# One core, eight batches of attention and experts: the first batch's loads and sums in another order

## The chip, the core and the metric

The kernel runs on one core of a Trainium2 chip. A core has TensorE (PE, matmuls; its weight loads are shown apart as PEld), VectorE (DVE), ScalarE (ACT), GpSimd (POOL) and SyncE (SP). SyncE here only issues DMA transfers; ScalarE issues a few at the start. Each queue works in its own order, and waits at an instruction until all that it needs is there. The metric is the device time of one execution in microseconds (us), as a median of several runs.

## What is computed

For each of 8 batches and 8 heads, 576 positions are mapped onto 32 memory slots by a softmax of `phi`; keys and values of the slots are weighted sums over the positions; each query attends to the 32 slots. The heads side by side make a token of 512 numbers. A router picks one of 8 experts for each token, and the expert is two matrices with a ReLU between, scaled by the router's probability.

```python
a = softmax(phi, axis=2)                       # [8, 8, 576, 32]
k_m = einsum('bhsm,bhsd->bhmd', a, k)          # 32 slots of 64 for each head
v_m = einsum('bhsm,bhsd->bhmd', a, v)
x = softmax(q @ k_m.T / 8) @ v_m               # then [4608, 512]
logits = unit(x) @ unit(expert_emb).T / tau
e, gate = argmax(logits), max(softmax(logits))
out = gate * (relu(x @ w1[e]) @ w2[e])         # all in float32
```

## The kernel before

The host lays the inputs out: `phiT` has 4 heads times 32 slots on 128 partitions (two groups `g` of four heads), `kv` holds keys and values of 512 positions side by side, and `kvt` those of the last 64.

The program is written out by hand; every engine gets its instructions in the order of the code, and nothing reorders them. For each batch b:

- `load_phi` brings the two maps (288 KB each) to `ex`. `largest` takes the negated maximum of a row on VectorE (L393), `softmax` the exponential on ScalarE with its sum (L407), `shares` the reciprocal of the sums on VectorE (L418, L422).
- `turn` transposes the exponentials on TensorE in blocks of 128 positions (L428), and ScalarE copies them to `eT` (L429).
- `load_kv` brings keys and values: four pieces of 128 positions, `kx0` to `kx3`, 512 KB each, and the last 64 positions, `kl`, 256 KB on 64 partitions.
- `slots(b, g)` sums them on TensorE: for one group of heads, five pieces k = 0 to 4 of four products each into one accumulator (L440). Group 0 of the first batch has the accumulator `acc`, group 1 another, `acc1`.
- `block` scales the sums with the shares, keys to `kb` (VectorE, L459), values to `vb` (ScalarE, L461). `flip` transposes them (L469) and copies them to `kT` and `vT` (L472). `score` then multiplies keys and queries (L485); `load_q` has brought the queries in two halves of 576 KB, the first for group 0 and the second for group 1.
- `Tokens` turns scores into attention, tokens and the choice of an expert: `fill`, `weigh`, `divide`, `turn`, `attend`, `choose`. The chosen expert's `w1` and `w2` are loaded only then (L378, L384).
- `project`, `first` and `second` are the expert's matmuls, and most of TensorE's work. The next batch's steps are threaded between them by `steps`.

For the first batch there is nothing to thread into. The entry function writes its steps one after the other: `warm` keeps TensorE busy with matmuls of a constant, then loads, constants, softmax and the router (a generator in three parts: the square of the embedding on ScalarE, a square root by iteration on VectorE, the transposes on TensorE). The DMA issues of the start stand on two queues: SyncE has the maps, `kx0` to `kx3`, then the queries; ScalarE has `kl`, the embedding `emb` and `tau`. The program gives its DMA transfers eight semaphores in turn, so that the ninth waits for the first to land: here `kx3` waits for `kl` (L359).

## Time and profile before

| what | us |
|---|---|
| three runs | 423.91, 424.69, 425.17 |
| median | 424.69 |
| the profiled execution | 424.73 |
| its span, first to last instruction | 422.9 |
| TensorE busy in it | 406.7 |

Times in the rows below are microseconds from the start of the span, of the one profiled execution. A row of the timeline has start, duration, engine, line, operation, what it writes and reads with shapes, how many instructions were merged (x4), and in brackets the idle time of the engine before it and what ended that. A letter q behind an engine (SPq, ACTq) marks its queue issuing a DMA; the landing comes later. Matmuls in float32 take several passes and are recorded more than once each.

### The profile page before, as it was taken

The page shows a single profiled execution, that of the slowest core. Times are in us where ns is not written, and L with a number is a line of the kernel's source. Part 1 is how long each engine was busy: PE and PEld are TensorE (multiplying, and loading weights), DVE is VectorE, ACT ScalarE, POOL GpSimd, SP SyncE. Part 2 cuts the span into 40 slices and gives each one's busy share as a digit, 9 for nine tenths or more (in the row PEclk, how much of TensorE's full clock was granted, in tenths as well). Part 3 has the DMA queues.
Part 4 walks back from the last instruction along what each step waited for, and adds up shares of the span by engine and source line. Part 5 has one row for each costly group of instructions (what it writes and reads, how often), then busy time and mean ns, then how long its engine had stood idle before and what let it go on. Part 6 is the DMA issues. An engine that isn't in the chain of part 4 may idle for free. (4 is left out here: it accounts for less than half of the span.)

```text
span 422.9 us, 9359 instructions
## 1 busy us (share of the span) xinstructions
PE 406.7 (96%) x3485; PEld 329.1 (78%) x3485; DVE 258.7 (61%) x830; ACT 169.2 (40%) x462; POOL 167.5 (40%) x195
## 2 busy tenths in 40 slices
PE   7779899999999999999999999999999999999994
PEld 2448778688887978879786888879788797869784
DVE  5698796569673695547772696736955476645000
ACT  4465732365223632257313652236322571045110
POOL 1021471295133921268131951339212681339100
PEclk9999999999999999999999999999999999999998
DMA  8989925996769924995469926699349504592011
GB/s 264 354 320 338 359 60 134 315 348 246 154 202 405 330 48 112 352 359 222 69 195 379 340 109 146 209 404 331 50 112 345 193 2 87 163 380 69 15 50 55
DMA packets 67570, 91.19 MB, mean 216 GB/s; under 512 B 40792, under 2 KB 45656, under 8 KB 67520
## 3 DMA queue, kind: packets, MB, share of 16 engines
q1 hardware_dynamic: 64720, 82.00, 58.8%
q0 software_dynamic: 2688, 8.26, 5.5%
q8 instruction: 29, 0.48, 0.4%
q10 hardware_dynamic: 112, 0.28, 0.2%
q14 instruction: 21, 0.17, 0.1%
HBM read 71.19 MB, written 19.33 MB: 214 GB/s over the span
## 5 line engine op out<-in xcount | busy, mean ns | idle before, releaser
L579 PE MATMUL ph<-aT,gh 128*128 128x288 f32 x512 | 105.7, 300 | 1.7 <-DVE hl L585 1.1
L632 PE MATMUL py<-wh,hh 128*128 128x512 f32 x248 | 102.0, 411 | 0.0
L632 PE MATMUL py<-wh,hl 128*128 128x512 f32 x248 | 97.1, 391 | 0.0
L632 PE MATMUL py<-wl,hh 128*128 128x512 f32 x248 | 96.8, 390 | 0.0
L550 POOL TENSOR_TENSOR wl<-w2s,wh 128x512 fp32r<-128x512 f32 x64 | 83.4, 1306 | 19.1 <-DMA kx<-kv 12.7
L579 PEld LDWEIGHTS ph<-aT,gh 128*128 128x128 f32 x512 | 81.3, 188 | 5.6 <-DVE gl L563 2.6
L579 PE MATMUL ph<-aT,gl 128*128 128x288 f32 x256 | 75.3, 294 | 0.0
L585 DVE SCALAR_TENSOR_TENSOR hl<-ph,hh 128x288 fp32r<-128x288 f32 x128 | 55.7, 449 | 28.0 <-ACT hh L582 21.2
L637 ACT ACTIVATE ys<-py,gate 128x512 f32<-128x512 f32 (+1 forms) x39 | 25.0, 640 | 107.9 <-PE py L632 50.9
L582 ACT ACTIVATE hh<-ph 128x288 fp32r<-128x288 f32 x128 | 51.7, 416 | 30.0 <-PE ph L579 28.3
L736 POOL DMA_DIRECT2D out_dram<-ys x28 | 15.5, 553 | 109.2 <-ACT ys L637 101.6
L632 PEld LDWEIGHTS py<-wh,hh 128*128 128x128 f32 x248 | 46.6, 188 | 12.1 <-issue 4.3
L632 PEld LDWEIGHTS py<-wh,hl 128*128 128x128 f32 x248 | 46.5, 188 | 10.2
L632 PEld LDWEIGHTS py<-wl,hh 128*128 128x128 f32 x248 | 46.7, 188 | 8.1
L579 PEld LDWEIGHTS ph<-aT,gl 128*128 128x128 f32 x256 | 48.0, 188 | 0.0
L540 POOL TENSOR_TENSOR aT<-aw,aT 128x576 fp32r<-128x576 f32 (+3 forms) x20 | 23.8, 1205 | 48.8 <-PE py L632 35.8
L563 DVE TENSOR_TENSOR gl<-pg,gh 128x512 fp32r<-128x512 f32 x32 | 20.0, 684 | 36.3 <-ACT gh L562 36.2
L549 POOL CAST wh<-w2s 128x512 fp32r<-128x512 f32 x56 | 37.5, 670 | 0.0
L621 PE MATMUL py<-w2s,h 128*64 128x256 f32 x256 | 29.4, 382 | 0.0
L119 DVE TENSOR_REDUCE lg<-po 128x8 f32<-128x16 f32 x40 | 6.8, 174 | 30.4 <-PE po L114 30.4
L621 PEld LDWEIGHTS py<-w2s,h 128*64 128x64 f32 x256 | 17.7, 137 | 9.3 <-issue 1.3
L114 PEld LDWEIGHTS po<-vv,aw 128*128 128x128 f32 x160 | 21.8, 189 | 3.5 <-ACT vv L526 1.0
(154 smaller groups left out, 506.2 us busy)
## 6 DMA issues: line engine op xcount, KB each, us to landing
kx<-kv SPq DMA_DIRECT2D x32, 512.0 KB, 7.3
w2s<-w SPq DMA_DIRECT2D x32, 512.0 KB, 9.8
w1s<-w SPq DMA_DIRECT2D x28, 512.0 KB, 5.2
qt<-qT SPq DMA_DIRECT2D x14, 576.0 KB, 7.7
out_dram<-ys POOLq DMA_DIRECT2D x28, 256.0 KB, 6.0
ex<-phiT SPq DMA_DIRECT2D x16, 288.0 KB, 10.1
ad<-aw SPq DMA_DIRECT2D x8, 576.0 KB, 12.6
td<-x SPq DMA_DIRECT2D x56, 72.0 KB, 2.2
```

The source lines that it names most:

```text
L114: nc.tensor.matmul(po[:, 144 * g : 144 * g + P + E], lhsT=k.aw[:, g, to], rhs=k.vv[:, g], start=True, stop=True)
L540: self.nc.gpsimd.tensor_tensor(out=al, in0=a, in1=ah.bitcast(F32), op=ALU.subtract)
L549: (copy or self.nc.scalar.copy)(h, x)
L550: self.nc.gpsimd.tensor_tensor(out=l, in0=x, in1=h.bitcast(F32), op=ALU.subtract)
L563: nc.vector.tensor_tensor(out=self.gl[:, g, f], in0=ps[g], in1=self.gh[:, g, f].bitcast(F32), op=ALU.subtract)
L579: nc.tensor.matmul(p, lhsT=w[:, g, fs], rhs=x[:, g, to], start=g == 0 and k == 0, stop=g == 1 and k == 2)
L582: nc.scalar.activation(self.hh[:, f, to], p, AF.Relu)
L585: nc.vector.scalar_tensor_tensor(out=self.hl[:, f, to], in0=p, scalar=0.0, in1=self.hh[:, f, to].bitcast(F32), op0=ALU.max, op1=ALU.subtract)
L621: nc.tensor.matmul(p[64 * j : 64 * j + 64], lhsT=self.h4[:, f], rhs=self.w2s[:, f, d * j : d * j + d], start=f == 0, stop=f == 7,)
L632: nc.tensor.matmul(p, lhsT=h[:, f, to], rhs=w[:, f], start=f == 0 and k == 0, stop=f == 7 and k == 2)
L637: nc.scalar.activation(y[:, :d], p, AF.Copy, scale=gate[:, i : i + 1])
L736: eng.dma_start(self.out[r : r + P], y)
```

## The change

It touches the first batch alone.

- The loads: `load_router` (emb, tau) is issued ahead of keys, values and queries. The keys and values follow in it: `kx1` on ScalarE's queue, `kx0`, `kx2`, `kx3` and then `kl` on SyncE's. Queries come after that.
- An exponential of one constant per partition is put on ScalarE behind its loads, so that the table of exponentials is loaded there.
- The router's square comes ahead of the exponentials, its square root ahead of the shares. Both maxima are taken before either share, and the shares of both groups after the transposes, with one reciprocal.
- The sums of both groups are interleaved by piece: pieces 0 and 1 of group 0, then of group 1, then piece 2 of both, piece 3 of both, piece 4 (`kl`) of both. Both `block` steps come behind that.

```diff
@@ load_router
         nc.scalar.dma_start(self.tv, self.tau.broadcast_to((E, 1)))
+        self.load_kv(0)
+        nc.scalar.activation(st([P, 1], F32, name="e8"), self.ones[:, :1], AF.Exp)
@@ load_kv
-        if b < B:
-            (self.nc.sync if b else self.nc.scalar).dma_start(self.kl[:64], self.kvt[b])
+        if not b:
+            for k in range(4):
+                (self.nc.scalar if k == 1 else self.nc.sync).dma_start(self.kx[k], self.kv[b, :, k])
+            self.nc.sync.dma_start(self.kl[:64], self.kvt[b])
+        elif b < B:
+            self.nc.sync.dma_start(self.kl[:64], self.kvt[b])
             for k in range(4):
                 self.nc.sync.dma_start(self.kx[k], self.kv[b, :, k])
@@ slots
-    def slots(self, b, g, acc=None):
+    def slots(self, b, g, acc=None, ks=(0, 1, 2, 3, 4), start=True, stop=True):
...
-        for k in range(5):
+        for k in ks:
...
-                    start=k == 0,
-                    stop=k == 4,
+                    start=start and k == ks[0],
+                    stop=stop and k == ks[-1],
@@ moe_linformer
     k.load_phi(0)
-    k.load_kv(0)
+    k.load_router()
     k.load_q(0)
-    k.load_router()
     k.consts()
...
     router = k.router()
+    next(router)
     for g in range(NG):
+        k.largest(0, g)
         k.softmax(0, (g,))
-        k.shares(0, (g,))
     next(router)
...
+    k.shares(0)
     k.load_phi(1)
-    next(router)
...
-    k.slots(0, 0)
+    for ks in ((0, 1), (2,), (3,), (4,)):
+        for g in range(NG):
+            k.slots(0, g, acc if g else None, ks, start=0 in ks, stop=4 in ks)
     k.block(0, 0)
-    k.slots(0, 1, acc)
```

In the order of the instructions, two places change. The first is the head of SyncE's queue, here with the semaphores that an issue waits for (`DMAHW0` to `DMAHW7` are the eight of the DMA transfers). Before:

```order
L353 DMA ex<-phiT 128x576 x2
L359 DMA kx_70<-kv 128x1024
L359 DMA kx_71<-kv 128x1024
L359 DMA kx_72<-kv 128x1024
L359 DMA kx_73<-kv 128x1024 [waits DMAHW0_49]
L366 DMA qt<-qT 128x1152 [waits DMAHW1_49]
L366 DMA qt<-qT 128x1152 [waits DMAHW2_49]
```

and in the changed kernel:

```order
L355 DMA ex_69<-phiT 128x576 x2
L360 DMA kx0_70<-kv 128x1024
L360 DMA kx2_72<-kv 128x1024
L360 DMA kx3_73<-kv 128x1024
L361 DMA kl_74<-kvt 64x1024 [waits DMAHW0_49]
L372 DMA qt_75<-qT 128x1152 [waits DMAHW1_49]
L372 DMA qt_75<-qT 128x1152 [waits DMAHW2_49]
```

`kx1` has left this queue and `kl` has come to the end of the keys; `DMAHW0` is `kl`'s own in the kernel before and `emb`'s in the changed one. The queries stand behind both as they did. ScalarE's queue, before, up to the square of the router (L321):

```order
L357 DMA kl<-kvt 64x1024
L311 DMA sT<-emb 8x512
L313 DMA tv<-tau 8x1
L407 ACT_TABLE_LOAD
L407 ACTIVATE ex,sm_149<-ex,nm_148 128x576 x2
L321 ACTIVATE w2s,es<-sT 8x512
```

and in the changed kernel:

```order
L311 DMA sT<-emb 8x512
L313 DMA tv<-tau 8x1
L360 DMA kx_71<-kv 128x1024
L315 ACT_TABLE_LOAD
L315 ACTIVATE e_129<-ones 128x1
L323 ACTIVATE w2s,es<-sT 8x512
L413 ACTIVATE ex,sm_153<-ex,nm_152 128x576 x2
```

The table load has moved from behind the wait for the first map to behind the issues, and the square from behind the exponentials to ahead of them. The second place is on TensorE, the products of the first batch (`acc` is group 0's accumulator, `acc_146` or `acc_148` group 1's; each row is four products). Before:

```order
L440 MATMUL acc<-kx_70,eT 32x128 x4
L440 MATMUL acc<-kx_71,eT 32x128 x4
L440 MATMUL acc<-kx_72,eT 32x128 x4
L440 MATMUL acc<-kx_73,eT 32x128 x4
L440 MATMUL acc<-kl,eT 32x128 x4
L440 MATMUL acc_146<-kx_70,eT 32x128 x4
L440 MATMUL acc_146<-kx_71,eT 32x128 x4
L440 MATMUL acc_146<-kx_72,eT 32x128 x4
L440 MATMUL acc_146<-kx_73,eT 32x128 x4
L440 MATMUL acc_146<-kl,eT 32x128 x4
```

and in the changed kernel:

```order
L446 MATMUL acc<-kx_70,eT 32x128 x4
L446 MATMUL acc<-kx_71,eT 32x128 x4
L446 MATMUL acc_148<-kx_70,eT 32x128 x4
L446 MATMUL acc_148<-kx_71,eT 32x128 x4
L446 MATMUL acc<-kx_72,eT 32x128 x4
L446 MATMUL acc_148<-kx_72,eT 32x128 x4
L446 MATMUL acc<-kx_73,eT 32x128 x4
L446 MATMUL acc_148<-kx_73,eT 32x128 x4
L446 MATMUL acc<-kl,eT 32x128 x4
L446 MATMUL acc_148<-kl,eT 32x128 x4
```

The products are the same forty; those of group 1 have come from behind all of group 0's to right behind its product of the same piece.

## Rows read from the trace of the kernel before

**Rows 1.** The head of the profile's page: the span.

```profile
span 422.9 us, 9359 instructions
```

**Rows 2.** The table by stretch for the first 14 us and for one stretch of the steady part: from and to, its length, then the busy time of each engine (x instructions), the granted clock of TensorE, the busy share of the DMA engines and GB/s.

```profile
0.00:14.00 14.00, 9.89 (x104) 4.83 (x105) 7.30 (x32) 5.31 (x11) 1.73 (x8) 1.00 0.87 302
101.00:152.00 51.00, 51.00 (x445) 41.66 (x446) 33.15 (x105) 20.46 (x57) 21.52 (x24) 1.00 0.70 231
```

**Rows 3.** The waits of TensorE over the whole run, longest in total first: who waited, for whom, us in total, times, the longest.

```profile
PE acc L440 <- DMA kx<-kv: 2.2, 4, 0.9
...
PE ph L579 <- DVE hl L585: 1.1, 1, 1.1
...
PE pg L560 <- DMA w1s<-w: 0.7, 1, 0.7
```

**Rows 4.** The timeline of the first batch, from the first loads to the scores of the second group.

```profile
0.71 0.55 ACTq L357 DMA_DIRECT2D kl<-kvt  x1
...
1.30 0.72 ACTq L311 DMA_DIRECT2D sT<-emb  x1
...
3.86 0.75 DVE L393 TENSOR_REDUCE nm<-ex 128x1 f32<-128x576 f32 x1 [0.85 <-DMA ex<-phiT]
3.91 1.28 ACT L407 ACT_TABLE_LOAD   x1 [3.91 <-DMA ex<-phiT]
...
5.20 0.77 ACT L407 ACTIVATE ex<-ex,nm 128x576 f32<-128x576 f32 x1
...
6.37 0.73 DVE L393 TENSOR_REDUCE nm<-ex 128x1 f32<-128x576 f32 x1
...
7.91 0.62 ACT L321 ACTIVATE w2s<-sT 8x512 f32<-8x512 f32 x1
...
9.13 0.43 PE L440 MATMUL acc<-kx,eT 128*32 128x128 f32 x8 [0.31 <-ACT eT L429]
...
9.75 0.43 PE L440 MATMUL acc<-kx,eT 128*32 128x128 f32 x8 [0.18 <-DMA kx<-kv]
...
11.17 0.47 DVE L328 TENSOR_SCALAR w2s<-sT,en 8x512 f32<-8x512 f32 x1
...
12.27 0.43 PE L440 MATMUL acc<-kx,eT 128*32 128x128 f32 x8 [0.85 <-DMA kx<-kv]
...
12.52 0.40 PE L440 MATMUL acc<-kl,eT 128*32 128x128 f32 x8
...
12.73 1.06 PE L440 MATMUL acc<-kx,eT 128*32 128x128 f32 x32
...
14.08 0.48 DVE L459 TENSOR_SCALAR kb<-acc,rs 128x256 f32<-128x256 f32 x1 [0.61 <-PE acc L440]
...
14.62 0.44 PE L469 MATMUL tf_1True<-ident,kb 128*128 128x128 f32 x2 [0.25 <-DVE kb L459]
...
14.99 0.85 PE L485 MATMUL ts<-qt,kT 64*32 64x128 f32 x16
15.10 0.27 ACT L472 COPY kT<-tf_1True 128x128 f32<-128x128 f32 x1 [0.42 <-PE tf_1True L469]
...
15.42 0.15 PEld L485 LDWEIGHTS ts<-qt,kT 64*32 64x32 f32 x8 [0.27 <-ACT kT L472]
```

**Rows 5.** The table by stretch again (columns as in rows 2), for what the DMA engines moved: before the first maps, up to the landing of `kx3`, right after it, a later stretch with a `kl` in flight, and the stretch behind that.

```profile
0.00:2.00 2.00, 0.97 (x3) 0.42 (x4) 1.11 (x6) 0.00 (x0) 1.36 (x8) 1.00 0.15 26
...
2.00:12.27 10.27, 7.19 (x46) 2.87 (x44) 5.71 (x27) 4.83 (x10) 0.38 (x1) 1.00 0.99 337
...
12.00:14.00 2.00, 1.73 (x57) 1.53 (x58) 0.48 (x1) 0.47 (x1) 0.00 (x0) 1.00 1.02 418
...
40.50:44.00 3.50, 3.50 (x66) 2.88 (x66) 3.19 (x19) 1.84 (x7) 0.00 (x0) 1.00 1.05 244
44.50:48.00 3.50, 2.71 (x21) 2.47 (x19) 2.53 (x8) 3.50 (x15) 1.52 (x2) 1.00 1.02 404
```

**Rows 6.** From issue to landing in us, from the lists of DMA issues and of single tiles: `kl` of the first batch, `kl` of the third; the issue of the two halves of the queries on SyncE's queue; the landing of the first half alone; and shortest, median and longest of the two halves, the longest being the second's.

```profile
kl<-kvt ACTq DMA_DIRECT2D x1, 256.0 KB, 4.7
...
kl<-kvt SPq DMA_DIRECT2D x1, 256.0 KB, 10.9
...
5.75 1.28 SPq L366 DMA_DIRECT2D qt<-qT  x2
...
qt<-qT SPq DMA_DIRECT2D x1, 576.0 KB, 7.9
...
DMA to landing us min/median/max: 7.9/8.3/8.7
```

**Rows 7.** The timeline where the chosen expert's first matrix is issued and where TensorE takes up its second half.

```profile
22.45 1.42 SPq L378 DMA_DIRECT2D w1s<-w  x2
...
31.78 1.09 PE L560 MATMUL pg<-w1s,vT 64*32 64x512 f32 x16 [0.67 <-DMA w1s<-w]
```

**Rows 8.** The timeline of VectorE near 47 us.

```profile
46.47 1.26 DVE L220 TENSOR_SCALAR zz<-zz 128x5 f32<-128x5 f32 x1
```

**Rows 9.** The table by stretch (columns as in rows 2) for a stretch of the start in which TensorE stands idle, and for the end, behind the last matmul.

```profile
24.67:26.00 1.33, 0.00 (x1) 0.00 (x1) 1.06 (x4) 1.33 (x5) 0.00 (x0) 1.00 1.03 363
417.12:419.00 1.88, 0.00 (x1) 0.00 (x0) 0.48 (x1) 0.00 (x0) 0.00 (x0) 1.00 0.22 73
419.00:420.00 1.00, 0.00 (x0) 0.00 (x0) 0.00 (x0) 0.00 (x0) 0.00 (x0) 0.70 0.08 18
```

## The prediction, written before the changed kernel ran

> **What bounds the kernel now.** I first read the span and the table by stage: in the steady part TensorE is busy for 51 us of 51, while the first 14 us leave it 4.1 us idle [rows 1, 2]. So an edit of the first batch can only make the steady part begin earlier or later. The chain that ended last holds one piece, at the very end, and says nothing of the start; the list of waits does. TensorE's longest are those on the keys and values (2.2 us), then one on VectorE's hl (1.1 us) and one on w1 (0.7 us) [rows 3]. In order of time, TensorE has the transposed exponentials at 9.13 and then stands before each piece of keys and values: kx1 at 9.75, kx3 at 12.27. The second group's sums run only after that, its kb is made at 14.08, its keys are turned at 14.62, its copy kT ends at 15.37 (15.10 and 0.27), and the scores of the second group, ts, start at 15.42 [rows 4].
>
> What the keys wait for is bytes, not issue: between 2.00 and 12.27 us the DMA engines are busy for 0.99 of the time at 337 GB/s, and at 418 from 12 to 14 us [rows 5]. Those 10.27 us moved 3.46 MB; maps, keys and values and embedding are 2896 KB, 2.97 MB. So the moved bytes are 0.5 MB, or 1.2 us at 418 GB/s, ahead of what has landed.
>
> One load stands close behind: the second half of q was issued at about 6.4 us (two issues in 1.28 us from 5.75) and took 8.7 us, so it landed at 15.1 us [rows 6]. The scores that need it began at 15.42. That is 0.3 us of slack, and this number decides my forecast.
>
> **The change part by part.** *Exponentials.* The table load of 1.28 us stood at 3.91, behind the wait for the maps, and the first exponential came at 5.20 [rows 4]. In front of it ScalarE now issues three loads, at most 0.72 us each (emb's), and then loads the table: 0.71 + 2.2 + 1.28 = 4.2 us at the latest, before the first maximum can be ready (3.86 + 0.75 = 4.6). An exponential of one element per partition is new, between 0 and the 0.27 us of a 128x128 copy, also before the maximum. The router's square, 0.62 us, now goes ahead of the exponentials instead of behind them, so the first starts at about 5.1, as before or a little earlier. It waits for emb to land, which no row of before shows; even at 7 us both exponentials, 0.77 each, would end before 9.75. The second maximum (6.37) stood behind the first share; it now waits for its map alone, so it is not later. With the square gone from between, the copies of the transposes come about 0.6 us earlier. All of this is covered by kx1, which came at 9.75 [rows 4]: I price it at 0; without that cover it would be 0.3 us, the wait on eT at 9.13, since the next wait is for keys anyway.
>
> *Router and shares.* VectorE's router chain ended at 11.64 (11.17 and 0.47) and now goes ahead of the shares (five small adds and one reciprocal, under 1 us). It could not start before the square's end at 8.5; now it starts once the square and the second maximum are done, by 7.1 (6.37 and its 0.73), 1.4 us earlier, so it ends near 10.2 and the shares are ready near 11.2. Their reader kb cannot run before the last load has landed, at 12.3 (below) [rows 4]. Cover of 1 us, cost 0; at L = 10.3, the low bound below, it would cost 0.9. One reciprocal less on VectorE: 0, off the path.
>
> *Queues.* kx1 moves from SyncE's queue to ScalarE's, kl from the head of ScalarE's to the end of the keys on SyncE's. SyncE's stall at the fourth key load, which waited until kl had landed (0.71 + 4.7 = 5.4), is gone; kl waits for emb instead, and q's first half for the first map, landed at 3.86. With the engines at 0.99 busy, earlier issue moves no byte earlier: 0. The Trainium skill's page "DMA: Bandwidth & Descriptors" (section "Issuing engines are not separate DMA queues") says the same against this edit: loads of several queues run on the same engines, and a second queue saves the issue time alone. The busy share here agrees.
>
> *Order of the sums.* The work of TensorE is the same, but after the last landing L only the kl products of both groups remain. Eight rows took 0.40, and 32 took 1.06, so about 0.27 per group: both done at L + 0.7. Then VectorE makes both kb, 0.48 each, from L + 0.45 to L + 1.45; the turn takes 0.44 and ScalarE's copy 0.27, with waits as before, so ts of the second group may start at L + 2.3. In the old order it started 15.42 - 12.27 = 3.15 after its last landing [rows 4]. That alone is a gain of 0.85 us, if L stays at 12.3.
>
> *L.* The bytes up to kl are those that had landed by 12.27, so I take L = 12.3. Below: all at 418 GB/s gives 2.0 + 7.1 + 1.2 = 10.3. Above: kx3 lands 0.63 earlier (256 KB at 418 GB/s) and kl, which landed 3.4 us after the engines began (0.71 + 4.7 = 5.4; 26 GB/s up to 2 us), takes these 3.4 by itself: 15.0 [rows 4 to 6]. Stretches with a kl in flight are slow, 244 GB/s from 40.5 to 44 against 404 right after, and the kl of a later batch took 10.9 us [rows 5, 6]; this keeps me from the low end, but the same slow stretch is in the 337 GB/s already. The Trainium skill's page "SBUF — State Buffer" (section "Door 1: The DMA port swizzle") says that 64 partitions, which is what kl fills, reach half of the memory's ports and get about 196 GB/s. By that page kl would take, as an estimate, 1.3 us in place of 0.63, L would be near 13.0 and the gain in the sum below 0.1 in place of 0.3; the slow stretches agree in kind.
>
> *q.* It stays behind the same bytes, so it lands at 15.1 again; from 13.0 (4.15 MB at 418 GB/s, 2.0 + 9.9 + 1.1) to 15.7 (0.6 us more, if the slow stretch is longer in its new place) [rows 5, 6].
>
> *Sum.* The second ts starts at the later of L + 2.3 = 14.6 and q = 15.1, so at 15.1 in place of 15.42: a gain of 0.3. With the bounds: 13.0 to 17.3, from 2.4 faster to 1.9 slower.
>
> *To the end.* The scores lead over VectorE's chain to the choice of an expert and so to the issue of w1 (22.45); the second half of w1 lets the projection start at 31.78, where TensorE waited 0.67 us [rows 7]. From there the order fixes the rest. SyncE's later issues (the next batch's keys, released at 14.07 by the last products) come about 1 us earlier; nobody on the path waits for them. So 0.3 us arrives at the end. The profiled execution took 424.73, of which 422.9 is span; 424.73 - 0.3 = 424.4. The median of the three runs, 424.69, is the same within 0.04.
>
> **The rivals.** *A: the DMA gets faster.* If kl at the head of the line is what slowed phi and the keys, everything lands sooner; q at 13.8 and L at 11.5 would give ts at 13.8, a gain of 1.6: 423.1. For it: 337 against 418 GB/s, and the slow stretches go with kl [rows 5]. Against it: kl is still ahead of q, so its slow stretch should only move.
>
> *B: the last load becomes the bound, slower.* kl lands after all keys. From L = 13.1 on, L + 2.3 is later than 15.42 and the change loses. With kl needing its 3.4 us alone, L = 15.0 and the loss is 1.9: 426.6. For it: the 10.9 us of the later kl [rows 6]. Against it: the first kl shared its 3.4 us with both maps, the later one with all that stood ahead in the queue.
>
> *C: the change does nothing.* Its gains are all under the DMA or fall to q, or the keys of the next batch or w1 hold the start in place: 424.7.
>
> *D: the clock.* TensorE would stand idle between the products of kx3 and the landing of kl. The granted clock stayed at 1.00 over an idle stretch of 1.33 us and fell within 419 to 420, some 2 us after the last matmul [rows 9]. If it fell from 2.4 to 1.2 GHz here, the 2.0 us of matmuls from L to the end of ts (0.7, 0.44, 0.85) would take twice as long: +2.0 - 0.3, 426.4. By bytes the idle stretch is about 1 us, so it is unlikely.
>
> *E: the stall at 48 us.* A 128x5 add took 1.26 us on VectorE near 47 us, and TensorE then waited 1.1 us for hl [rows 3, 8]. If a shift of the start breaks up that meeting, 1.1 us come back: 423.3.
>
> **How the numbers follow.** Forecast (gain 0 to 1.0, q bounds) 0.58, A 0.17, B 0.08, C 0.08, D 0.03, E 0.06. About 0.3%, 1.27 us, is what a measurement of this kernel can tell from no change. Faster by that: most of A (0.14), half of E and a small tail of the forecast, 0.20 in all; slower by that: B from L = 14.4 on (0.03), D (0.03) and a tail, 0.08; within it 0.72. For 8 in 10 the range takes the forecast, C, E and the inner part of A and of B: 422.9 to 425.5.
>
> **What would show it.** Right: exponentials end by 7.5; the products of kl are the last for both groups, within 0.8 us; the second ts starts near 15.1 and its wait is on the DMA of q, no longer on ScalarE's copy; w1 is issued near 22.1. A shows itself by q landing before 14.2 and over 380 GB/s from 2 to 12 us; B by kl landing after 13.1 with TensorE waiting for kl longest; D by a granted clock under 1.00 before 20 us; E by no wait on hl near 48. I am wrong if the second ts starts before 14.4 or after 15.6, or if it starts near 15.1 and the span moves by over 1 us all the same.

## The result: 0.75% slower, where a gain of 0.3 us was forecast

| | kernel before | changed kernel |
|---|---|---|
| median, us (18 runs each) | 424.56 | 427.88 |
| lowest to highest | 423.49 to 426.21 | 424.54 to 430.10 |
| the profiled execution | 424.73 | 428.48 |
| its span | 422.9 | 426.7 |

The ratio is 1.0075 with an interval of 1.0054 to 1.0096: slower, outside the range of 422.9 to 425.5.

TensorE's mean granted clock is known for each run (0.988 for the profiled one), and it counts below: a run with 0.994 or more is taken as one in which the clock held through the batches, one with 0.993 or less as one in which it fell for some microseconds. The line is a rough one. The profiles show where the clock was at half: behind the last matmul it takes 0.001 to 0.0065 off the mean of a run, with no cost in the batches, and a fall of 3.4 us within the batches takes only 0.004 (e6's profiled run, counted as held with 0.994, has one). So the counts of falls below are counts by this line. Of the changed kernel's 18 runs 4 held, with a median of 425.43, and 14 fell, with 428.39. The forecast said 424.4. One run of the kernel before, 511.66 us at a clock of 0.75, is left out everywhere.

The head of the changed kernel's page, for [rows 1]:

```profile
span 426.7 us, 9361 instructions
```

Its longest waits of TensorE (who waited, for whom, us in total, times, the longest), for [rows 3]:

```profile
PE acc L446 <- DMA kx<-kv: 2.8, 2, 1.9
PE acc L446 <- ACT vb L467: 1.8, 1, 1.8
PE acc L446 <- DMA kl<-kvt: 1.3, 1, 1.3
PE ph L585 <- DVE hl L591: 1.1, 1, 1.1
...
PE pg L566 <- DMA w1s<-w: 0.9, 1, 0.9
```

A wait on kl, which no row of before has, and a longer one on the keys. Where they lie, the timeline of its first batch tells, for [rows 4]:

```profile
1.63 1.37 SPq L360 DMA_DIRECT2D kx<-kv  x3
...
2.04 1.28 ACT L315 ACT_TABLE_LOAD   x1 [2.04 <-issue]
...
3.04 0.58 SPq L361 DMA_DIRECT2D kl<-kvt  x1
...
4.34 0.77 ACT L413 ACTIVATE ex<-ex,nm 128x576 f32<-128x576 f32 x1 [0.20 <-DVE nm L399]
...
5.52 0.78 ACT L413 ACTIVATE ex<-ex,nm 128x576 f32<-128x576 f32 x1 [0.31 <-DVE eng L38]
...
8.78 1.64 PE L446 MATMUL acc<-kx,eT 128*32 128x128 f32 x48 [0.90 <-DMA kx<-kv]
...
12.32 0.64 PE L446 MATMUL acc<-kx,eT 128*32 128x128 f32 x16 [1.90 <-DMA kx<-kv]
...
14.25 1.08 PE L446 MATMUL acc<-kl,eT 128*32 128x128 f32 x16 [1.29 <-DMA kl<-kvt]
14.97 0.93 DVE L465 TENSOR_SCALAR kb<-acc,rs 128x256 f32<-128x256 f32 x2 [5.79 <-PE acc L446]
...
15.99 0.65 PE L475 MATMUL tf_1True<-ident,kb 128*128 128x128 f32 x2
...
16.67 0.27 ACT L478 COPY kT<-tf_1True 128x128 f32<-128x128 f32 x1 [0.17 <-PE tf_1True L475]
...
16.99 0.20 PEld L491 LDWEIGHTS ts<-qt,kT 64*32 64x32 f32 x8 [0.23 <-ACT kT L478]
```

(acc<-kx and acc<-kl are the products of the sums, kb the scaled keys, tf their transposes, kT the copies of these, ts the scores.) The exponentials are through at 6.3, earlier than before. Then TensorE has the first three pieces from 8.78 on, stands 1.90 us for kx3 and 1.29 us for kl, which comes at 14.25. The second group's scores start at 16.99 in place of 15.42, and wait for the copy kT, not for q. The products of kl took 1.08 us; the same sixteen rows took 0.64 in e2 below, where the clock held. The table by stretch, for [rows 2, 5, 9] (from and to, length, busy time of PE, PEld, DVE, ACT, POOL, granted clock, DMA share, GB/s):

```profile
2.00:12.27 10.27, 7.52 (x70) 4.15 (x68) 5.57 (x26) 5.28 (x11) 0.38 (x1) 1.00 0.99 319
10.00:12.00 2.00, 0.42 (x16) 0.15 (x8) 0.00 (x0) 0.00 (x0) 0.00 (x0) 1.00 1.03 214
12.00:14.00 2.00, 0.64 (x16) 0.38 (x16) 0.00 (x0) 0.00 (x0) 0.00 (x0) 0.88 0.99 297
13.50:20.30 6.80, 5.88 (x60) 3.29 (x68) 3.48 (x8) 2.50 (x9) 0.00 (x0) 0.50 0.95 288
20.30:22.00 1.70, 1.70 (x31) 0.90 (x16) 1.58 (x6) 1.03 (x5) 0.00 (x0) 0.98 1.03 417
```

From 10 to 12 us, with kl in flight behind the keys, the DMA engines are as busy as before and move 214 GB/s, where 12 to 14 us had 418 in the kernel before [rows 5]. TensorE is idle for 2.9 of the 4 us from 10 to 14, and its granted clock goes to 0.50 (1.2 GHz) from 13.5 to 20.3, while kl's products, the transposes and the scores run.

The way on, for [rows 7]: the issue of w1, the projection with its second half (pg), and the first products of the expert's first matrix (ph), which stood at 32.80 in the kernel before:

```profile
24.67 1.40 SPq L384 DMA_DIRECT2D w1s<-w  x2
...
34.38 1.09 PE L566 MATMUL pg<-w1s,vT 64*32 64x512 f32 x16 [0.91 <-DMA w1s<-w]
...
35.40 0.53 PE L585 MATMUL ph<-aT,gh 128*128 128x288 f32 x2
```

So 2.60 of the 3.75 us of the profiled executions are lost before the first ph. The rest: the steady batches take 49.35 us each in place of 49.30, from the start of the same product of the expert's second matrix (py) in the second and the seventh batch, (347.51 - 101.00) / 5 in the kernel before and (350.52 - 103.75) / 5 in the changed one:

```profile
101.00 0.44 PE L621 MATMUL py<-w2s,h 128*64 128x256 f32 x2
...
347.51 0.44 PE L621 MATMUL py<-w2s,h 128*64 128x256 f32 x2
```

```profile
103.75 0.44 PE L627 MATMUL py<-w2s,h 128*64 128x256 f32 x2
...
350.52 0.44 PE L627 MATMUL py<-w2s,h 128*64 128x256 f32 x2
```

With the first and the last batch that makes 0.4; the last matmul starts 3.02 us later (416.84 and 419.86). The remaining 0.7 lies behind it: the span ends 6.1 us after the last matmul's start in the kernel before and 6.8 in the changed one. In the profiles of all the kernels below this end took 6.1 to 8.1 us.

### The profile page after: what moved, and what is told of

It is laid out like the page before. It is cut to its first block, busy times and chain, and to the rows that moved or that the text cites. A ratio compares the mean times of both kernels' runs of the same rounds, so it can differ in the third digit from the quotient of the medians.

```text
span 426.7 us, 9361 instructions
## 1 busy us (share of the span) xinstructions
PE 408.8 (96%) x3485; PEld 331.1 (78%) x3485; DVE 257.9 (60%) x829; ACT 169.5 (40%) x463; POOL 167.5 (39%) x195
## 5 line engine op out<-in xcount | busy, mean ns | idle before, releaser
L638 PEld LDWEIGHTS py<-wh,hh 128*128 128x128 f32 x248 | 46.6, 188 | 12.3 <-issue 4.3
L638 PEld LDWEIGHTS py<-wh,hl 128*128 128x128 f32 x248 | 46.5, 188 | 10.2
## 6 DMA issues: line engine op xcount, KB each, us to landing
ex<-phiT SPq DMA_DIRECT2D x16, 288.0 KB, 10.3
```

The source lines that it names most:

```text
L638: nc.tensor.matmul(p, lhsT=h[:, f, to], rhs=w[:, f], start=f == 0 and k == 0, stop=f == 7 and k == 2)
```

## The experiments

Each was timed beside the kernel before on its own chip. That kernel's median there was 425.1 to 426.5, and by the line above 56 of its 135 runs fell (median 426.4 to 427.1 on the chips) and 79 held (424.8 to 425.0). So the two kinds of run lie some 1.6 to 2.3 us apart, and both happen to the kernel before too. Some expectations put the line at 0.996, which also counts runs as fallen whose only stretch at half clock is the end: e12's profile has a mean of 0.995 and 1.00 all through the start. Ratios are to the kernel before; 95% intervals stand in brackets.

### Where kl stands

**e1_kl_first**: the changed kernel with kl at the head of ScalarE's queue.

```diff
-            self.nc.sync.dma_start(self.kl[:64], self.kvt[b])     # load_kv, b == 0
...
     k.load_phi(0)
+    k.nc.scalar.dma_start(k.kl[:64], k.kvt[0])
     k.load_router()
```

> The changed kernel with one part undone: kl is issued at the head of ScalarE's queue again, all else stays (kx1 on ScalarE's queue, sums by piece, router and exponentials as changed). Theory 1 (kl's place: its slow flight, put behind the keys, makes kx3 and kl late, and the idle TensorE then loses its clock): no landing after 12.6 us, TensorE never idle for more than 1.5 us before the last products, granted clock 1.00 throughout the start, second group's scores start near 15.2, 424.3 us, the same as before or up to 0.5 below. Theory 2 (the sums by piece leave TensorE idle, whatever the order of the loads): the clock falls to 0.5 here too, 426.5 or more. Theory 3 (the second queue for kx1 upsets the order of the landings): kx3 lands at 12 or later with over 2 us between kx2 and kx3, 425.5 or more.

Measured: 426.24, ratio 1.0020 (0.9995 to 1.0046). No wait on kl is left, w1 is issued at 22.39 and the first ph starts at 32.62 in place of 35.40. A new wait came: emb stood behind kl, the square waited for it ahead of the exponentials, and TensorE waited 1.6 us for the exponentials:

```profile
5.92 0.63 ACT L323 ACTIVATE w2s<-sT 8x512 f32<-8x512 f32 x1 [1.62 <-DMA sT<-emb]
```

4 of 12 runs fell, beside 13 of 32 of the kernel before.

**e3_old_kl_last**: the kernel before with nothing changed but kl's place, behind kx3 on SyncE.

```diff
-            (self.nc.sync if b else self.nc.scalar).dma_start(self.kl[:64], self.kvt[b])
             for k in range(4):
                 self.nc.sync.dma_start(self.kx[k], self.kv[b, :, k])
+            if not b:
+                self.nc.sync.dma_start(self.kl[:64], self.kvt[b])
```

> The kernel before with one part of the change alone: kl is issued behind kx3 on SyncE's queue; sums, router and exponentials as before, one queue for the keys. Theory 1: kx3 near 12.3, kl near 14.2, and as the second group's products all come behind kl's, the second group's scores start near 17.3, 1.9 us late; with the clock held 426.6, with the clock lost 428 to 429. Theories 2 and 3 (sums by piece, second queue): neither is in here, so 424.6 and a clock of 1.00.

Measured: 429.24, ratio 1.0069 (1.0043 to 1.0096); all 9 runs fell. Its TensorE:

```profile
13.48 0.66 PE L443 MATMUL acc<-kx,eT 128*32 128x128 f32 x8 [2.03 <-DMA kx<-kv]
14.77 0.65 PE L443 MATMUL acc<-kl,eT 128*32 128x128 f32 x8 [0.63 <-DMA kl<-kvt]
```

That one line alone loses as much as the whole change. Note kx3: it comes 1.21 us later than in the kernel before, though it is now ahead of kl. So a kl in flight slows what flies with it; from 12 to 14 us the DMA moved 211 GB/s here.

**e4_kl128**: the changed kernel with the same 256 KB of kl laid on 128 partitions (four heads on each half), in all batches.

```diff
-        self.kl = st([P, H, 2 * D], F32, name="kl")
+        self.kl = st([P, 4, 2 * D], F32, name="kl")
...
-    a["kvt"] = kv[:, 512:]
+    a["kvt"] = kv[:, 512:].reshape(B, 64, 2, 4, 2 * D).transpose(0, 2, 1, 3, 4).reshape(B, P, 4, 2 * D)
```

> The changed kernel, but with the last 64 positions of keys and values laid out by the host on 128 partitions (heads 0 to 3 on the lower 64, heads 4 to 7 on the upper 64, 2 KB each) in all batches, their products over 64 partitions each; kl stays last in the queue. Theory 1 in its narrow form (the flight is slow because 64 partitions are written): no stretch under 300 GB/s between 5 and 14 us, kx3 near 11, kl before 12, q before 14.3, second group's scores near 14.3, clock 1.00: 423.4. If kl is slow for its place or its bytes and not for its partitions: landings as in the changed kernel, 427 to 428.

Measured: 427.48, ratio 1.0035 (1.0008 to 1.0062). Its TensorE in the first batch, and the DMA (columns as above):

```profile
11.20 0.64 PE L447 MATMUL acc<-kx,eT 128*32 128x128 f32 x16 [0.63 <-DMA kx<-kv]
12.23 0.45 PE L447 MATMUL acc<-kl,eT 64*32 64x128 f32 x16 [0.39 <-DMA kl<-kvt]
...
15.20 0.57 PE L492 MATMUL ts<-qt,kT 64*32 64x128 f32 x8 [0.72 <-DMA qt<-qT]
```

```profile
10.00:12.00 2.00, 1.21 (x32) 0.67 (x32) 0.00 (x0) 0.00 (x0) 0.00 (x0) 1.00 1.01 405
```

The slow stretch is gone (405 in place of 214 GB/s), kl comes at 12.23 in place of 14.25, and the second scores start at 15.20, waiting for q: the forecast's own picture. Nothing is gained all the same: 9 of 12 runs fell, and each later batch is 0.22 us longer (49.57 for 49.35). The edit also halves the height of kl's products and the size of its tile; which of these lengthens the batches is not shown.

### TensorE's gaps and the clock

**e2_warm**: the changed kernel with eight matmuls of the constant behind kx2's products and five behind kx3's.

```diff
+        k.warm({2: 8, 3: 5}.get(ks[0], 0), hot)
```

> The changed kernel with 8 matmuls of the constant put behind the products of kx2 and 5 behind those of kx3, into a tile that nobody reads, so that TensorE is not idle there. Theory 1: the granted clock stays at 1.00, kl still lands near 14.2, the second group's scores start near 16.5 in place of 15.42, and about 1.1 us of the loss stay: 425.7. So the clock would be about 2.2 us of the 3.3 us. If the clock is the whole loss (theory 2): 424.3 to 424.6. If the clock costs nothing: 427.9 as in the changed kernel.

Measured: 427.33, ratio 1.0036 (1.0007 to 1.0066); 3 of 12 runs fell in place of 14 of 18. In the profile the clock held, kl came at 14.24 as in the changed kernel, and the first ph started at 33.95:

```profile
14.24 0.64 PE L447 MATMUL acc<-kl,eT 128*32 128x128 f32 x16
...
33.95 0.40 PE L586 MATMUL ph<-aT,gh 128*128 128x288 f32 x1
```

Against 32.80 and 35.40 that parts the 2.60 us of the profiles: 1.15 from the landing, 1.45 from the clock. The medians need not part in the same way: the changed kernel's held and fallen runs lie 2.96 us apart, and e2's held runs have 426.72, the changed kernel's 425.43 on another chip.

**e5_before_warm**: more of these matmuls in the gaps of the kernel before.

```diff
-            k.warm(2)
+            hot = k.warm(4)
...
-    k.slots(0, 0)
+    for n in range(5):
+        k.slots(0, 0, ks=(n,), start=n == 0, stop=n == 4)
+        k.warm((0, 3, 3, 0, 0)[n], hot)
```

> The kernel before with more matmuls of the constant: four in place of two behind the first transposes, and three each (0.22 us a piece) behind the first batch's products of kx1 and kx2, where TensorE waited 0.82 and 0.85 us for the next load. Nothing else differs. Theory one, that TensorE's gaps are what lets the granted clock fall: the runs with a mean clock of 0.996 or more, half of 32 for the kernel before on the second chip, become nearly all, and the median goes down to that of the held runs, 424.96 against 425.82, a ratio near 0.998. Rival one, that the fall is a matter of chance whatever TensorE does: the same share of falls, ratio 1.000. Rival two, that the added matmuls stand in the way: kx3's products start after 12.5 in place of 12.27 us and the ratio is over 1.000.

Measured: 425.35, ratio 1.0000 (0.9978 to 1.0022). 1 of 12 runs fell, beside 11 of 29 of the kernel before; kx3's products came no later (12.15 for 12.27), and w1 was issued at 22.32 for 22.45. These 12 runs alone leave room for chance, but e2 above, and e10 below with 0 of 13 where e7 has 7 of 7, say the same. So the gaps bear on how often the clock falls, and rival one is out. The time that this should have given did not show: the runs that held have 425.35 beside 424.83. Part of that is the end (6.8 us behind the last matmul's start, 6.1 before); why it differs stays open.

### The other parts alone

**e6_sums_only**: the kernel before with the sums by piece, kl first.

```diff
-    k.slots(0, 0)
+    for ks in ((4,), (0,), (1,), (2,), (3,)):
+        for g in range(NG):
+            k.slots(0, g, acc if g else None, ks, start=4 in ks, stop=3 in ks)
     k.block(0, 0)
-    k.slots(0, 1, acc)
...
```

> The kernel before with one part of the change alone: the sums of both groups interleaved by piece, with kl, which is still loaded first, as the first piece. Theory (the prediction's step on the sums, with kl out of the way): no load lands later than before, kx3's products for both groups are the last, and the second group's ts starts at the later of kT and q, 15.1 to 15.2 in place of 15.42, waiting for q; 0.2 to 0.3 us faster where the clock holds. TensorE is a little busier between the pieces (0.53 in place of 0.27 us of products each) so that the clock should fall no more often than before. Rival: the interleaving itself costs, as the changed kernel's first projection came 2.6 us later: the second ts after 15.6.

Measured: 424.62, ratio 0.9988 (0.9969 to 1.0007), and the row of the second scores:

```profile
15.35 0.42 PE L485 MATMUL ts<-qt,kT 64*32 64x128 f32 x8 [0.83 <-DMA qt<-qT]
```

The forecast's mechanism: kT is ready 0.8 us before q, and q takes all of the gain but 0.07 us in this profile (15.35 for 15.42). By the line 2 of 12 runs fell. The profiled run counts as held, but its clock was at half behind the scores, and its first ph came at 33.29 for 32.80:

```profile
16.10:19.40 3.30, 3.30 (x38) 1.45 (x38) 3.01 (x10) 1.39 (x7) 0.00 (x0) 0.50 1.02 339
```

**e7_exps_only**: the kernel before with emb and tau first, the table load, the square, the maxima and the shares as in the change; kl stays at the head of the keys and the sums group by group.

```diff
+        self.load_kv(0)
+        nc.scalar.activation(st([P, 1], F32, name="e8"), self.ones[:, :1], AF.Exp)
...
-    k.load_kv(0)
+    k.load_router()
     k.load_q(0)
-    k.load_router()
...
+    next(router)
     for g in range(NG):
+        k.largest(0, g)
         k.softmax(0, (g,))
-        k.shares(0, (g,))
...
+    k.shares(0)
     k.load_phi(1)
-    next(router)
```

> The kernel before with the other part alone: emb and tau loaded first, the exponential of a constant and its tile of 4 bytes per partition, the router's square ahead of the exponentials, both maxima first, the shares behind the transposes. kl stays at the keys' head on ScalarE's queue, the sums stay group by group. The prediction's step gives 0 for it: the first products still wait for the keys, the second ts starts at 15.4. Theory two, that the added tile, which moves the tiles laid out after it, costs 0.05 us in each later batch: the period of the steady batches is 49.35 us in place of 49.30, and the kernel is 0.3 us slower with everything at the start as before. Rival: the period stays at 49.30, and the 0.05 us come from the order of the sums or the clock.

Measured: 428.27, ratio 1.0066 (1.0046 to 1.0086), all 7 runs fell: a part priced at 0 loses nearly as much as the whole. The last transposes of the kernel before, and then e7's TensorE and the clock behind it:

```profile
8.06 0.76 PE L428 MATMUL te<-ident,ex 128*128 128x128 f32 x5 [0.61 <-ACT ex L407]
```

```profile
6.61 0.82 PE L430 MATMUL te<-ident,ex 128*128 128x128 f32 x6
9.79 0.43 PE L442 MATMUL acc<-kx,eT 128*32 128x128 f32 x8 [2.36 <-DMA kx<-kv]
...
13.54 0.65 PE L442 MATMUL acc<-kx,eT 128*32 128x128 f32 x8 [0.86 <-DMA kx<-kv]
```

```profile
12.60:22.80 10.20, 9.34 (x121) 5.55 (x118) 4.50 (x12) 2.71 (x10) 0.00 (x0) 0.50 0.80 281
```

The transposes end 1.4 us earlier and win nothing, since the keys are not there; TensorE stands still for 2.36 us in one piece. The keys also come 1.2 to 1.3 us later (kx3 at 13.54 for 12.27), so some of that piece is theirs. The edit that bears on them is kl's issue, at 1.67 in place of 0.71, behind emb and tau; no run moves kl back alone. The period of the later batches is 49.34 us.

**e10_exps_warm**: e7 with constant matmuls in the gaps and without the added tile.

```diff
-        nc.scalar.activation(st([P, 1], F32, name="e8"), self.ones[:, :1], AF.Exp)
+        nc.scalar.activation(self.kT[:, 0, :1], self.ones[:, :1], AF.Exp)
...
+    k.warm(9, hot)                                # behind the transposes
...
+        k.warm((3, 3, 3, 0, 0)[n], hot)           # behind each piece of group 0
```

> The part on exponentials and router alone, which was slower by 0.66%, with two of its three suspected costs taken away: nine constant matmuls behind the transposes and three behind each of the first three pieces fill TensorE's gaps, and the constant's exponential is written into a tile that exists, so that no tile is added. The third stays: kl is issued 0.95 us later than in the kernel before, behind emb and tau, and the keys landed 1.25 us later each. Theory: three costs that add up; the granted clock holds in nearly all runs, the period of the steady batches is 49.30 us again, and what is left is the 1.25 us of the keys: the second ts near 16.6, first ph near 34.0, about 425.9 where the kernel before has 424.5 with the clock held and 425.4 over all its runs, a ratio near 1.001 to 1.002. Rival one: with kl later the clock is not the matter, the runs stay near 428. Rival two: the late keys were an effect of something else and the median falls to that of the kernel before or under it.

Measured: 425.82, ratio 1.0005 (0.9983 to 1.0028); none of 13 runs fell. The first ph starts at 33.99, 1.19 later than in the kernel before, which is the keys' lateness, and the same two products as above give (350.18 - 103.64) / 5 = 49.31 us for a batch:

```profile
103.64 0.44 PE L624 MATMUL py<-w2s,h 128*64 128x256 f32 x2
...
350.18 0.44 PE L624 MATMUL py<-w2s,h 128*64 128x256 f32 x2
```

All three costs are as the theory had them, up to the first ph and in the period. The profiled run is the slowest of the 13 (428.12), and it lost 1.9 us more between the first ph and the last matmul than the kernel before, outside these five batches; what did that is not shown. In every profile with the added tile the period is 49.34 to 49.36 (e4 apart), in every one without it 49.30 to 49.31.

### The second queue

**e11_queue**: the kernel before with kx1 on ScalarE's queue.

```diff
-                self.nc.sync.dma_start(self.kx[k], self.kv[b, :, k])
+                (self.nc.sync if b or k != 1 else self.nc.scalar).dma_start(self.kx[k], self.kv[b, :, k])
```

> The kernel before with the second queue alone: kx1 is issued on ScalarE's queue, behind kl and ahead of emb; all else as it was. The prediction's step on the queues gives 0: the DMA engines are busy with what was issued, so the pieces land in the same order within 0.3 us, kx1's products start near 9.75, kx3's near 12.3, the second ts near 15.4, ratio 1.000. Rival: two queues let kx1 and kx0 share the engines, so that kx0 lands later, and the first products wait beyond 9.13 with TensorE idle in one piece of over 0.5 us; or emb, issued later, holds up the router.

Measured: 424.69, ratio 0.9982 (0.9957 to 1.0006). The first ph starts at 31.74, and kx3's products 1.02 us earlier than in the kernel before, although the first products began at 10.13 in place of 9.13 (the second map's maximum waited for its map until 7.25):

```profile
11.25 0.43 PE L440 MATMUL acc<-kx,eT 128*32 128x128 f32 x8 [0.26 <-DMA kx<-kv]
```

**e13_one_queue**: the changed kernel with kx1 back on SyncE's queue.

```diff
-                (self.nc.scalar if k == 1 else self.nc.sync).dma_start(self.kx[k], self.kv[b, :, k])
+                self.nc.sync.dma_start(self.kx[k], self.kv[b, :, k])
```

> The changed kernel with kx1 back on SyncE's queue; all else of the change stays. Theory, that the second queue is a gain inside the change, as it was when made alone (kx3's products at 11.25 in place of 12.27): here the keys and kl land up to 1.0 us later than in the changed kernel, kl near 15.2 in place of 14.25, first ph later by as much, and the loss grows from 0.75% to about 1.0%. Rival, the prediction's step: the second queue is worth nothing with the DMA engines busy, kl lands at 14.25 again, and the loss stays at 0.7 to 0.8%.

Measured: 428.11, ratio 1.0038 (1.0014 to 1.0062), 10 of 12 runs fell. In the profile kx3 came at 13.48 for 12.32, kl at 14.80 for 14.25, the first ph at 36.97 for 35.40. The profile is with the theory as far as the landings go (its clock was at half for 10.2 us, the changed kernel's for 6.8); the ratio did not grow, but it was taken on another chip, and its interval meets that of the changed kernel.

**e14_two_pieces**: as e11, with kx2 on ScalarE's queue too.

```diff
+                (self.nc.sync if b or k not in (1, 2) else self.nc.scalar).dma_start(self.kx[k], self.kv[b, :, k])
```

> The kernel before with two pieces, kx1 and kx2, issued on ScalarE's queue behind kl; all else as it was. With kx1 alone there the keys landed 1.0 us earlier and the median was 0.45 us lower (interval 0.43% faster to 0.06% slower). Theory, that the shares of two queues are what helps (less waiting between one piece and the next): kx3's products start at 11.3 or earlier again, second ts near 14.4, ratio 0.997 to 0.999. Rival, that the earlier landing was chance from one execution to another: kx3's products start at 12.2 to 12.5 as in the profiles of the kernels with all keys on SyncE's queue, ratio 1.000.

Measured: 428.26, ratio 1.0035 (1.0014 to 1.0057). Neither theory: emb stood behind both pieces, the router's square waited for it, and the copies of the transposes stand behind the square:

```profile
11.44 0.63 ACT L321 ACTIVATE w2s<-sT 8x512 f32<-8x512 f32 x1 [2.75 <-DMA sT<-emb]
```

### Versions meant to win

**e8_both**: sums by piece, matmuls in the gaps, and the first 128 columns of q loaded ahead of the rest.

```diff
+                for m in (slice(P), slice(P, S)):
+                    self.nc.sync.dma_start(self.qt[:, :, m], self.qT[b, :, :, m])
```

> A version meant to beat both: the kernel before, sums of both groups interleaved by piece in the order kx0, kx1, kl, kx2, kx3 (kl is loaded first, as before), four constant matmuls behind the first transposes and one to three in the gaps ahead of kx2 and kx3, and the first batch's queries loaded as the first 128 columns of both groups (256 KB), then the rest. No added tile. Theory: kx3 lands at 12.3 as before, both groups' products end near 12.9, kb of the second near 13.7, its kT near 14.4, and q no longer bounds: the second ts starts near 14.5 in place of 15.42, w1 is issued near 21.6, the clock holds in nearly all runs; 0.9 us less than the held runs of the kernel before, 1.5 to 1.8 less than its median where half of its runs fall: a ratio of 0.996. Rival one: the load of w1 stays where it was because the next batch's loads stand ahead of it, and the first projection starts at 31.8 all the same: ratio 0.998 by the clock alone. Rival two: the queries' short rows slow the loads, and the second ts starts at 15.4 or later.

Measured: 426.65, ratio 1.0025 (1.0011 to 1.0039). The scores came as forecast, the second group's at 14.74; w1 did not (23.04). The next bound was close behind, the next batch's map, whose maximum stands in VectorE's row ahead of this batch's sums. 3 of 12 runs fell, and the held ones have 426.64, where the kernel before has 424.83:

```profile
17.64 0.75 DVE L398 TENSOR_REDUCE nm<-ex 128x1 f32<-128x576 f32 x1 [1.18 <-DMA ex<-phiT]
```

**e9_map_first**: e8 with that map issued ahead of q and its maximum taken early.

```diff
-    k.load_q(0)
     k.consts()
...
     k.load_phi(1)
+    k.load_q(0)
...
+    k.largest(1, 0)
     first, others = slice(0, 4), slice(4, BL)
```

> The version with sums by piece, added constant matmuls and the queries' first 128 columns loaded first, and one more step: the next batch's maps are issued ahead of all queries of the first batch, and VectorE takes the first of their maxima (0.75 us) ahead of the scores instead of between the scores' exponential and their sum, where it waited 1.18 us for that map. Theory: the map lands at 13.8, the 128 columns at 14.4, the maximum runs in VectorE's idle time before 14.8; the second ts starts near 14.7 as before this step, the sum z near 17.0 in place of 18.31, w1 is issued near 21.5 in place of 23.04 (22.45 in the kernel before), the first ph starts near 31.9 in place of 32.80; with the clock held, 0.9 us less than the held runs of the kernel before, a ratio of 0.995 to 0.997 to all of its runs. Rival one: w1 lands no earlier, since the next batch's keys and values stand ahead of it in the DMA; the first ph stays at 32.5 or later and the ratio is 0.998 or more. Rival two: the rest of the queries lands too late and the scores of the rest (tr) wait, so that tl and po start later than in the kernel before.

Measured: 430.98, ratio 1.0132 (1.0092 to 1.0172). Rival two: the rest of q came behind, and TensorE stood 3.3 us before the rest of the scores; 5 of 6 runs fell:

```profile
19.37 0.99 PE L491 MATMUL tr<-qt,kT 64*32 64x448 f32 x16 [3.33 <-DMA qt<-qT]
```

**e12_mended** and **e15_emb_sync**: the kernel before with the second queue, sums by piece and matmuls in the gaps; e15 has emb and tau on SyncE's queue as well.

```diff
-                self.nc.sync.dma_start(self.kx[k], self.kv[b, :, k])
+                (self.nc.sync if b or k != 1 else self.nc.scalar).dma_start(self.kx[k], self.kv[b, :, k])
+                if not b and k == 0:              # e15 alone; emb, tau on nc.sync
+                    self.load_router()
...
+    for ks in ((0,), (1,), (4,), (2,), (3,)):
+        for g in range(NG):
+            k.slots(0, g, acc if g else None, ks, start=0 in ks, stop=3 in ks)
+        k.warm({4: 1, 2: 3}.get(ks[0], 0), hot)   # e15: {2: 2}
```

> A version meant to beat both, from the parts that did no harm: the kernel before with kx1 issued on ScalarE's queue behind kl, the sums interleaved by piece in the order kx0, kx1, kl, kx2, kx3, and constant matmuls in TensorE's gaps (four behind the first transposes, one behind kl's products, three behind kx2's). Queries and maps as in the kernel before. Theory: the keys land 1.0 us earlier, as with the second queue alone, kx3's products for both groups end near 11.9, the second ts starts at the later of kT, near 13.4, and q, 13.4 to 14.4; w1 is issued at 20.9 to 21.5 in place of 22.45, the first ph starts near 31.5 in place of 32.80, and the clock holds in most runs: 0.8 to 1.2 us less than the held runs of the kernel before and a ratio of 0.996 to its median. Rival: the load of w1 or of the next batch's keys becomes the bound, nothing is left of the gain behind the choice of the expert, ratio 0.999 or more.

> The kernel before with kl and kx1 on ScalarE's queue and emb and tau on SyncE's behind kx0, the sums by piece in the order kx0, kx1, kl, kx2, kx3, four constant matmuls behind the first transposes and two behind kx2's products. Where emb stood behind kx1, or behind kx1 and kx2, the router's square waited 0.78 and 2.75 us for it, and the copies of the transposes stand behind the square on ScalarE. Theory: with emb out of the line the square waits for nothing, eT is ready near 9.1, kx3's products for both groups end near 12.0, the second ts starts near 13.5 to 14.4 (q) in place of 15.42, w1 is issued near 21.3, and the median is 0.5 to 1.0 us under that of the kernel before, 0.997 to 0.999. Rival: the keys land no earlier than with one queue, kx3's products start at 12.2 or later, the second ts at 15.0 or later, ratio 1.000.

Measured: 426.58, ratio 1.0004 (0.9986 to 1.0021), and 425.67, ratio 0.9984 (0.9962 to 1.0006); no run of either fell. In both the square still waited for emb (0.78 and 0.55 us), so the products began at 9.78 and 9.82 in place of 9.13; w1 was issued at 22.40 and 21.75. e12's twelve runs, all counted as held, have the median of 426.58, where the kernel before has 424.92 in its held runs on that chip: in the profile the end took 2.0 us longer (8.1 for 6.1).

**e16_after_mended**: the changed kernel with kl at the keys' head, emb and tau on SyncE, the square behind the exponentials, no added tile, and matmuls in the gaps.

```diff
+            self.nc.scalar.dma_start(self.kl[:64], self.kvt[b])
             for k in range(4):
                 (self.nc.scalar if k == 1 else self.nc.sync).dma_start(self.kx[k], self.kv[b, :, k])
-            self.nc.sync.dma_start(self.kl[:64], self.kvt[b])
+                if k == 0:
+                    self.load_router()
+            self.nc.scalar.activation(self.kT[:, 0, :1], self.ones[:, :1], AF.Exp)
...
-    next(router)
     for g in range(NG):
         k.largest(0, g)
         k.softmax(0, (g,))
     next(router)
...
+    k.warm(4, hot)
     k.shares(0)
+    next(router)
...
```

> The changed kernel with the costs that the runs named taken away: kl back at the head of the keys, on ScalarE's queue, and kx1 behind it; emb and tau on SyncE's queue behind kx0; the router's square behind the exponentials again; the constant's exponential into a tile that exists; the order of the sums kx0, kx1, kl, kx2, kx3; four constant matmuls behind the transposes and two behind kx2's products. The early table load, both maxima first, the late shares, the second queue and the sums by piece stay. Theory, that the loss was kl's place, TensorE's gaps and the added tile, and nothing else: the period of the steady batches is 49.30 us, no wait for kl, second ts at 13.5 to 14.4, and the kernel is as fast as the one before or up to 1.0 us faster, 0.997 to 1.000. Rival: a part that stays (late shares, early exponentials) costs by itself, and the ratio is 1.002 or more.

Measured: 426.20, ratio 1.0016 (0.9997 to 1.0035), none of 12 fell, period 49.31, the first ph at 32.08, the last matmul 0.46 us earlier than in the kernel before. In the profile what was lost at the start is won back, and the end behind the last matmul, 8.0 us in place of 6.1, takes more than that. No version is shown to beat the kernel before; e6, e11 and e15 have the lowest ratios, and each interval holds 1.

## Why the prediction was wrong

- *L* is the step that failed first. It put the last landing at 12.3, by bytes. kx3 alone came at 12.32, and kl 1.9 us behind it at 14.2 (its products at 14.25), where the working of the upper bound has 0.63 us for kl's bytes. The bounds of *L*, 10.3 to 15.0, held; the point and the chance of 0.08 for what lies beyond 13.1 did not. e1 and e4 take this lateness away, by kl's place and by its layout, and e3 brings it about by kl's place alone. The rows were read and then argued away: the slow stretch was said to be "in the 337 GB/s already". It was, but at a place where TensorE had other work; at the keys' end nothing covers it. The Trainium skill's page "SBUF — State Buffer" (section "Door 1: The DMA port swizzle") would have put L near 13.0, by the prediction's estimate from its 196 GB/s (with a gain near 0.1, not below it). By the runs that is the right sign and too small; in e3 the load beside kl, kx3, came 1.2 us later as well.
- Rival B, with 0.08, was the mechanism. Its point (13.1) was passed, and its price holds: L + 2.3 gives 16.5, measured 16.99 at half the clock (in e2, at the full clock, the copy kT ended at 16.41). Its sign, kl as the longest wait, came only in part: kx3, flying beside kl, made TensorE wait 1.90 us and kl 1.29.
- Rival D, with 0.03, happened in 14 of 18 runs by the line. Its price of 2.0 us lies within what was measured (1.45 in the profiles, 1.6 to 2.3 between held and fallen runs of the kernel before, 2.96 between those of the changed kernel). Its chance was not: "an idle stretch of 1.33 us" held once in one profile and was taken for a rule. The gaps here were 1.90 and 1.29 us with 0.64 us of work between, and the forecast did not see that the clock falls in some executions of one kernel and not in others: by the line, in 56 of 135 runs of the kernel before as well.
- *Exponentials*, priced at 0 since they end early: they did, and in e7 the part was not free. Earlier transposes and later keys put TensorE's idle time into one piece ahead of the keys (2.36 us, all runs fell; with the gaps filled, in e10, none). In the changed kernel the piece ahead of the keys was 0.90 us, and e1, which keeps this edit, fell no more often than the kernel before (4 of 12, 13 of 32). So what this part cost in the changed kernel itself is not shown.
- *Router and shares* at 0 was right: kb waited only for the products, and the shares were ready before 9.2.
- *Order of the sums* and *Sum* were right where L holds: 15.20 in e4 and 15.35 in e6, both waiting for q, for 15.1 forecast. *q* in the changed kernel was late too: its second half was issued at 4.8, took 11.5 us and landed near 16.3, outside the forecast's 13.0 to 15.7, but before the copy kT (16.94), so it cost nothing.
- *Queues* at 0 is neither borne out nor refuted. With kl first and kx1 on a second queue the DMA moved 401 to 407 GB/s from 6 to 10 us in five profiles (e11, e12, e14, e15, e16) but 366 in e1, with one queue 343 to 406 in five (before, e5, e6, e8, e9), and the keys came 1.02 us earlier in e11. The Trainium skill's page "DMA: Bandwidth & Descriptors" (section "Issuing engines are not separate DMA queues") grants a second queue the issue time alone. By the row above, with three issues in 1.37 us, that is 0.46 us for one. Most profiles hint at more, the medians can't tell (interval to 1.0006); how much of it is chance between executions stays open.
- Not foreseen at all: the added tile, 0.05 us in each steady batch, some 0.3 in all. The step that failed here is the premise that an edit of the first batch can only shift the steady part. That it comes and goes with the tile is shown; how a tile of 4 bytes does it is not.
- A and E did not happen: 319 GB/s from 2 to 12.27 us, and the wait on hl is still 1.1 us.
- One reading was short: in TensorE's list of waits the second place before is a wait of 1.3 us on vb, in the next batch's sums, and not the one on hl. It grew to 1.8 us in the changed kernel:

```profile
PE acc L440 <- ACT vb L461: 1.3, 1, 1.3
```

## What to carry to other kernels

A load that slows the others belongs where the engines have other work, so weigh its place by what waits while it flies, not by bytes. An edit that makes an engine ready earlier for data that come no earlier only gathers its idle time, and on TensorE that can cost the clock, as e7 and e10 show: price the gap, and count falls over many runs, since one profile shows one execution. Behind each wait that is removed, look for the load that lands next (here q, then the next batch's map, then the rest of q).

## What was not expected of the hardware

- 256 KB on 64 partitions held the DMA at 201 to 214 GB/s for some 2 us (changed kernel, e2, e3) with a busy share of about 1; the same bytes on 128 partitions left it at 405.
- By the line above, the granted clock fell in 41% of the runs of an unchanged kernel, and in 1 of 61 runs of five kernels whose gaps held matmuls of a constant (e5, e10, e12, e15, e16). In three more with such matmuls it fell more often (e2 and e8: 3 of 12 each; e9, with an idle stretch of 3.33 us left, 5 of 6). With the line at 0.996 it is 81 of 135 and 22 of 61, so the size of the difference hangs on the line and its direction does not.
- The time from the last matmul's start to the end of the span was 6.1 to 8.1 us over the profiles, with nothing in it but the scaling and the transfer of the last output. Why it differs between kernels with the same last instructions is not shown.
